# Low parts of the MLP weights kept in DRAM, MLP sums added on GpSimd, and a written order for GpSimd and SyncE, in an attention block with a token-mixing MLP

## The chip, the cores and the metric

One core of one Trainium2 chip. The metric is the time of one execution on the device in microseconds; the rows below come from one profiled execution, in which times count from the first instruction (the span).

## The reference, cut to what matters

```
x:(1,2048,640)  wqkv:(640,1920)  wo:(640,640)  w1:(2048,1728)  w2:(1728,2048)
g = sigmoid((x * gate_w).sum(-1, keepdims=True))
qkv = x @ wqkv                       # 32 heads of 20
a = softmax(q k^T * 20**-0.5) v @ wo
h = layernorm(x)                     # over the 640 channels
u = gelu(einsum("bsd,sf->bdf", h, w1) + b1)
b = einsum("bdf,fs->bds", u, w2) + b2, transposed back to (1,2048,640)
out = g * a + (1 - g) * b
```

## The kernel before

Every float32 matrix product outside the attention weights is made of float32r parts. A value is split into a high part (a copy to float32r) and a low part (value minus high part) by `hi_lo`, and a product is the sum high x high, high x low, low x high. TensorE's order is written out (`manual_schedule`) for the whole kernel, that of ScalarE and VectorE from L212 to L664. GpSimd and SyncE get an order from the scheduler, which may place their instructions earlier or later than the program does.

The span falls into four parts. First come the projections: q and k are stored to DRAM as high and low parts (`qk_unit`), then v, and the statistics of x. The last 24 units of q and k (loop at L373) already run beside `h_load`, `h_norm` and `h_split`, which normalize x for the MLP, and beside the first four pieces of weights.

Then comes the MLP, `mlp`, in two halves of the channels (d = 0 and 1, 320 channels each). For each of 14 blocks f of the hidden width it makes `u` (2048 tokens in, four pieces of weights of four 128x128 tiles each), then for each of 16 blocks t of tokens it makes `y` (four pieces each). Each of the 2592 yields of `mlp` is one step: a pair of matmuls (`pair64`) of 64 contraction rows each, one into each of two PSUM tiles, so a result is the sum of two PSUM tiles. `u_evac` has ScalarE copy the first, and five steps later VectorE adds the second (L411); then ScalarE makes the gelu and the high part, GpSimd the low part. `y_evac` does the same with a scale and a bias (L438, L441) and has SyncE store the result to `y_d`.

The list `w_list` names the weights twice over, once for each half, 120 pieces for each. `w_need(k)` loads pieces up to k+8 on SyncE (`w_raw`, eight buffers) and splits pieces up to k+3 (`w_split`, five buffers of each part): the high part on ScalarE, the low part on GpSimd.

Meanwhile TensorE and VectorE also run a stream of score tiles (`s_tiles`), which finds the maximum of each row of scores before the softmax: a matmul into one of three PSUM buffers `s` and a VectorE reduction (L148) per tile, 128 tiles for each pair of heads p. 736 of the 2048 tiles are run within the MLP, evenly over its steps. After each 64 tiles the reductions are joined in four VectorE instructions in a row (L151 to L157) and stored to `m_d`. At the first tile of p, a hook (`start_ahead`) loads the stack of q and k rows for p+1 (`base_stack`: 18 loads), and at p = 4, tile 512, also the stack for the attention of p = 0 (20 loads), `load_m` (8) and `load_v` (1).

Then the attention: 16 pairs of heads by 32 iterations. An iteration makes four score tiles (`st_op`), a ScalarE exponential on each (L646), the products with v of the iteration before (`pv_flush`), and takes 0, 2 or 3 tiles of the stream between them. Last come the output projection and the store.

Of the kernel before, what the change touches and what calls it, by code (L numbers as in the profile page):

```python
# [7 lines left out]
F32 = mybir.dt.float32  # L8
F32R = mybir.dt.float32r
# [19 lines left out]
def gated_mix(ctx, tc, xT, x, wqk, wv0, wv1, wo, w1, w1t, b1, w2, b2, out):  # L29
# [63 lines left out]
    omg = cp.tile([P, NT], F32, name="omg")  # L93
    b2o = cp.tile([P, NT], F32, name="b2o")

    def load_stack(p, ks, qs, full):
        for j in range(2):
            r0 = 64 * j
            h = 2 * p + j
            rows = slice(DH * h, DH * h + DH)  # L100
            kf = ks.bitcast(F32)
            nc.sync.dma_start(kf[r0: r0 + DH, :], k_d[0, rows, :])
            nc.sync.dma_start(kf[r0 + DH: r0 + 2 * DH, :], k_d[0, rows, :])
            nc.sync.dma_start(kf[r0 + 2 * DH: r0 + 3 * DH, :], k_d[1, rows, :])
            if full:
                nc.sync.dma_start(kf[r0 + 3 * DH: r0 + 3 * DH + 2, :], ones)
            for i in range(2):
                qf = qs[i].bitcast(F32)
                cols = slice(i * (S // 2), (i + 1) * (S // 2))
                nc.sync.dma_start(qf[r0: r0 + DH, :], q_d[0, rows, cols])  # L110
                nc.sync.dma_start(qf[r0 + DH: r0 + 2 * DH, :], q_d[1, rows, cols])
                nc.sync.dma_start(qf[r0 + 2 * DH: r0 + 3 * DH, :], q_d[0, rows, cols])

    def base_stack(p, full):
        ks = k8([P, S], F32R, f"ks{p}_{full}")
        qs = [q4([P, S // 2], F32R, f"qs{p}_{full}_{i}") for i in range(2)]
        load_stack(p, ks, qs, full)
        return ks, qs

    def load_m(p, qs):  # L120
# [10 lines left out]
    def load_v(p):  # L131
        v_tiles[p] = base.tile([P, NT, NPAIR], F32, tag="v", bufs=2, name=f"v{p}")
        c0 = NPAIR * (p % 8)
        nc.sync.dma_start(v_tiles[p], v_d[p // 8, :, :, c0: c0 + NPAIR].rearrange("t p c -> p t c"))

    def s_tiles(p):
        for half in range(2):
            mx = cp.tile([P, 4, 2, 8], F32, tag="mx", bufs=2, name=f"mx{p}_{half}")
            for t in range(8):
                for kc in range(4):  # L140
                    for j in (1, 0):
                        def f(j=j, kc=kc, t=t):
# [7 lines left out]
            mm = cp.tile([P, 16], F32, tag="mm", bufs=2, name=f"mm{p}_{half}")  # L150
            nc.vector.tensor_reduce(mm, mx.rearrange("p k j t -> p (j t) k"), axis=AX.X, op=OP.max)  # L151
            mc = cp.tile([P, 32], F32R, tag="mc", bufs=2, name=f"mc{p}_{half}")
            mt = cp.tile([P, 32], F32, tag="mt", bufs=2, name=f"mt{p}_{half}")
            nc.vector.tensor_scalar_mul(mc[:, :16], mm, -1.0)
            nc.vector.scalar_tensor_tensor(mc[:, 16:], mm, -1.0, mc[:, :16].bitcast(F32),
                                           op0=OP.mult, op1=OP.subtract)
            nc.vector.transpose(mt, mc.bitcast(F32))  # L157
            m_queue[0].dma_start(m_d[p, half], mt)
# [168 lines left out]
    for _ in range(2):  # L327
        for f in f_order:
            for c in range(4):
                w_list.append((w1t[:, 4 * c: 4 * c + 4], True) if f == FF else (w1[f][:, 4 * c: 4 * c + 4], False))  # L330
        for t in range(NT):
            for c in range(4):
                w_list.append((w2[t][:, 4 * c: min(4 * c + 4, FT)], False))
    AHEAD = 4
    w_tmp = [k8([P, 16, P], F32R, f"wtmp{i}") for i in range(2)]
    w_raws, w_got = [], []
# [36 lines left out]
    for n, (m, q) in enumerate(units):  # L373
        if q == 0 and n + 4 < len(units):
            w[units[n + 4][0]] = load_w(units[n + 4][0])
        if n == 19:
            s_src[0] = base_stack(0, False)
# [9 lines left out]
        if n in (18, 19):  # L387
            w_split(n - 18)
            w_raw(n - 16)
        qk_unit(m, w[m], q)  # L390
        if n in (20, 21):
            w_split(n - 18)
    p1s.close()

    gps = ExitStack()
# [12 lines left out]
    def u_evac(f, d, ps, gh, gl):  # L408
        xg = gp.tile([P, HALF], F32, tag="xg", bufs=3, name=f"xg{d}_{f}")
        nc.scalar.activation(xg, ps[0], AF.Copy)  # L410
        soon.append([5, lambda: nc.vector.tensor_add(xg, ps[1], xg)])  # L411
        if f == FF:
            soon.append([6, lambda: u_swap(d, xg)])
# [8 lines left out]
    def u_swap(d, xg):  # L422
        sw = gp.tile([P, HALF], F32, tag="sw", bufs=1, name=f"sw{d}")
        nc.gpsimd.dma_start(sw[:TL], xg[TL:])
        nc.gpsimd.dma_start(sw[TL:], xg[:TL])
        nc.gpsimd.tensor_add(xg, xg, sw)

    def u_tail(f, d, xg, gh):
        nc.scalar.activation(xg, xg, AF.Gelu_apprx_tanh, bias=b1_t[:, f:f + 1])
# [5 lines left out]
    def y_evac(t, d, ps):  # L435
        ty = hp.tile([P, HALF], F32, tag="ty", bufs=3, name=f"ty{d}_{t}")
        c = slice(t, t + 1)
        nc.scalar.activation(ty, ps[0], AF.Identity, bias=b2o[:, c], scale=omg[:, c])  # L438

        def rest():  # L440
            nc.vector.scalar_tensor_tensor(ty, ps[1], omg[:, c], ty, op0=OP.mult, op1=OP.add)  # L441
            nc.sync.dma_start(y_d[t * P:(t + 1) * P, d * HALF:(d + 1) * HALF], ty)

        soon.append([5, rest])

    def mlp(hs):
        k = 0
# [59 lines left out]
    for n, _ in enumerate(steps):  # L507
        settle()
        while done + 2 <= S_AHEAD and done < S_AHEAD * (n + 1) / STEPS:
            for _ in range(2):  # L510
                next(stream)()
            done += 2
    settle(True)
    while done < S_AHEAD:
        next(stream)()
        done += 1
    gps.close()
    hps.close()
# [13 lines left out]
            s_src[p + 1] = s_stack(p + 1)  # L532

    hooks[0] = start_loop
    m_queue[0] = nc.gpsimd
    s_src[6] = s_stack(6)

    def norm_steps(h0, h1):
# [82 lines left out]
    for p in range(NP):  # L621
# [3 lines left out]
        for it in range(32):  # L625
# [23 lines left out]
            due = min((p * 32 + it + 1) * LEFT // (NP * 32 - 38) + 1, LEFT)
            take = min(due - given, 3)  # L650
            for n in range(4):
                st_op((n + turn) % 2, n // 2, s_tile if n == 0 and take < 3 else st_tile)
                if n < take:
                    next(stream)()
            given += take
            if take and given == LEFT:
                next(stream, None)
# [83 lines left out]
```

## Time and profile before

| | us |
|---|---|
| median of three runs | 1918.32 (1918.08 to 1920.92) |
| profiled execution, its own time | 1924.69 |
| span of the profiled execution | 1922.9 |
| TensorE busy in the span | 1878.7 (98%) |
| VectorE busy | 1463.1 (76%) |
| ScalarE busy | 1335.4 (69%) |
| GpSimd busy | 557.5 (29%) |

The matmuls' ends are modelled, so a busy share of TensorE near 100% is not its peak rate. Each of the four parts of the span has its own limit, and the shares of the whole span mix them.

### The profile page before, as it was taken

To read this page: it belongs to the slowest core of one execution; us is meant where nothing else is said; L and a number is where in the kernel's file an instruction comes from. 1 tells how busy PE (TensorE), PEld (TensorE's weight loads), DVE (VectorE), ACT (ScalarE), POOL (GpSimd) and SP (SyncE) were. 2 spreads that over 40 slices of the span, in tenths; PEclk is the share of its full clock that TensorE was granted. 3 is DMA by queue.
4 is the path that set the end of the run, shared out by engine and by line. 5 is a ranking of instruction groups with operands and counts; after the bars stand their busy time and mean duration, and the time that the engine had idled before them with its cause. 6 is when DMAs were issued, how large, how long until landed. Compare 5 with 4: busy or idle time off the path is not lost. (4 is left out here: it accounts for less than half of the span.)

```text
span 1922.9 us, 39183 instructions
## 1 busy us (share of the span) xinstructions
PE 1878.7 (98%) x14978; PEld 1162.0 (60%) x14978; DVE 1463.1 (76%) x2465; ACT 1335.4 (69%) x2595; POOL 557.5 (29%) x731
## 2 busy tenths in 40 slices
PE   9999889999999999999999999999999999999998
PEld 7998788998999996333333333333333333333378
DVE  4202388999999997888888888888888888886127
ACT  4253233343443335999999999999999999999930
POOL 1024266667776562210110101001220012111210
PEclk9999899999999998999999999999999999999999
DMA  8467775556655563315040404231542134211263
GB/s 282 139 198 220 208 180 153 148 162 175 171 141 142 163 177 93 80 40 113 7 97 12 99 16 89 53 84 24 107 101 69 32 76 99 48 34 52 70 217 134
DMA packets 153742, 216.63 MB, mean 113 GB/s; under 512 B 66783, under 2 KB 92991, under 8 KB 149647
## 3 DMA queue, kind: packets, MB, share of 16 engines
q1 hardware_dynamic: 136336, 186.96, 36.6%
q0 software_dynamic: 13472, 18.63, 4.3%
q10 hardware_dynamic: 3744, 8.52, 1.3%
q8 instruction: 118, 1.93, 0.5%
q14 instruction: 72, 0.58, 0.1%
HBM read 165.43 MB, written 48.25 MB: 111 GB/s over the span
## 5 line engine op out<-in xcount | busy, mean ns | idle before, releaser
L148 DVE TENSOR_REDUCE mx<-s 128x1 f32<-128x512 f32 x2048 | 1283.5, 683 | 168.8 <-PE s L146 149.5
L646 ACT ACTIVATE p<-st 128x512 f32<-128x512 f32 x2048 | 1050.8, 620 | 41.1 <-PE s L146 14.7
L643 PEld LDWEIGHTS st<-qs_True,ks_True 62*128 62x128 f32 x2048 | 326.5, 185 | 476.0 <-ACT p L646 229.8
L643 PE MATMUL st<-qs_True,ks_True 62*128 62x512 f32 x2048 | 606.5, 424 | 1.2 <-ACT p L646 0.8
L586 PE MATMUL pv<-p,v 128*32 128x512 f32 x4096 | 550.1, 606 | 0.0
L146 PE MATMUL s<-sk,sq 60*128 60x512 f32 x1280 | 442.2, 440 | 2.6 <-DVE mx L148 2.6
L41 POOL TENSOR_TENSOR wl<-wr,wh 128x512 fp32r<-128x512 f32 x228 | 271.8, 1215 | 117.4 <-ACT wh L38 100.2
L146 PE MATMUL s<-ks_False,qs_False 60*128 60x512 f32 x768 | 253.3, 411 | 11.7 <-DVE mx L148 11.7
L573 POOL DMA_DIRECT2D o_d<-oev x128 | 66.5, 519 | 611.4 <-DVE oev L567 593.3
L38 ACT ACTIVATE wh<-wr 128x512 fp32r<-128x512 f32 (+2 forms) x246 | 139.9, 594 | 137.0 <-PE y L46 50.4
L146 PEld LDWEIGHTS s<-sk,sq 60*128 60x128 f32 x1280 | 208.5, 184 | 21.6 <-DVE mx L148 12.7
L46 PE MATMUL y<-gh,wh 64*128 64x320 f32 x896 | 208.6, 310 | 0.0
L46 PE MATMUL u<-hh,wh 64*128 64x320 f32 x864 | 199.7, 310 | 4.4 <-ACT wh L38 4.4
L46 PE MATMUL y<-gh,wl 64*128 64x320 f32 x832 | 200.5, 310 | 2.7 <-POOL wl L41 2.7
L46 PE MATMUL y<-gl,wh 64*128 64x320 f32 x832 | 202.6, 310 | 0.0
L46 PE MATMUL u<-hl,wh 64*128 64x320 f32 x864 | 199.1, 309 | 0.0
L46 PE MATMUL u<-hh,wl 64*128 64x320 f32 x800 | 188.1, 311 | 4.5 <-POOL wl L41 4.5
L586 PEld LDWEIGHTS pv<-p,v 128*32 128x32 f32 x4096 | 83.0, 108 | 173.8 <-issue 162.1
L46 PEld LDWEIGHTS y<-gh,wh 64*128 64x128 f32 x896 | 154.3, 187 | 0.4
L146 PEld LDWEIGHTS s<-ks_False,qs_False 60*128 60x128 f32 x768 | 138.3, 188 | 24.9 <-DVE mx L148 23.4
L46 PEld LDWEIGHTS u<-hh,wh 64*128 64x128 f32 x864 | 150.0, 188 | 4.8 <-ACT wh L38 4.6
L46 PEld LDWEIGHTS u<-hl,wh 64*128 64x128 f32 x864 | 150.8, 188 | 0.3
(112 smaller groups left out, 1837.4 us busy)
## 6 DMA issues: line engine op xcount, KB each, us to landing
wr<-in_w_dram SPq DMA_DIRECT2D x200, 256.0 KB
qs_True<-q_d SPq DMA_DIRECT2D x192, 80.0 KB
ks_True<-k_d SPq DMA_DIRECT2D x96, 160.0 KB
sk<-k_d SPq DMA_DIRECT2D x60, 160.0 KB
sq<-q_d SPq DMA_DIRECT2D x120, 80.0 KB
qs_False<-q_d SPq DMA_DIRECT2D x72, 80.0 KB
ks_False<-k_d SPq DMA_DIRECT2D x36, 160.0 KB
v_d<-vt SPq DMA_DIRECT2D x32, 168.0 KB
```

The source lines that it names most:

```text
L38: nc.scalar.activation(hi, src, AF.Copy)
L41: (lo_eng or nc.vector).tensor_sub(lo, src, hi.bitcast(F32))
L46: nc.tensor.matmul(ps[k], a[r], b[r], start=start, stop=stop)
L146: nc.tensor.matmul(ps, qs[half][r, t * P:(t + 1) * P], ks[r, kc * 512:(kc + 1) * 512], start=True, stop=True)
L148: nc.vector.tensor_reduce(mx[:, kc, j, t: t + 1], ps, axis=AX.X, op=OP.max)
L573: nc.gpsimd.dma_start(o_d[DH * h: DH * h + DH, cols], ev[r: r + DH, :])
L586: nc.tensor.matmul(pv[r: r + 32, :], v_tiles[p][:, kt, 10 * j: 10 * j + 32], pts[j, c], start=(kt == 0), stop=(kt == NT - 1))
L643: nc.tensor.matmul(ps, ks[r, kt * P:(kt + 1) * P], qs[qh][r, c * 512:(c + 1) * 512], start=True, stop=True)
L646: nc.scalar.activation(pt, ps, AF.Exp, scale=SCALE)
```

## The change

ScalarE copies both PSUM tiles of an MLP sum to SBUF, and GpSimd adds the copies. In the second half of the channels, h_norm runs on ScalarE in two instructions. GpSimd, SyncE too, follow the program's order from the start of the projections' last loop to the end of the attention. In the first half, ScalarE's queue stores each low part of the weights to a DRAM tensor `lo_d`; in the second half SyncE loads it from there, and GpSimd makes none. The stores of `y_d` go to ScalarE's queue, 24 steps after the evacuation; those of `m_d` to GpSimd's. The joining of 64 reductions is spread: two tiles later the reduction on VectorE and negation and split on GpSimd, eight tiles later the transposition on VectorE. The loads of the first stack and the first four pieces go to GpSimd's queue, those of the stack for p = 1 to tile 48. In the attention, iterations that take two tiles of the stream order them differently, and the stream ends six iterations earlier.

```
 base_stack(p, full, eng=nc.sync), load_stack likewise: all loads go to eng
+def s_max(p, half, mx):
+    nc.vector.tensor_reduce(mm, mx.rearrange("p k j t -> p (j t) k"), axis=AX.X, op=OP.max)
+    nc.gpsimd.tensor_scalar_mul(mm, mm, -1.0)
+    hi_lo(mc[:, :16], mc[:, 16:], mm, hi_eng=nc.gpsimd, lo_eng=nc.gpsimd)
+    s_close.append([8, lambda: s_store(p, half, mc)])
+def s_store(p, half, mc):
+    nc.vector.transpose(mt, mc.bitcast(F32))
+    s_close.append([M_LAG[0], lambda: m_queue[0].dma_start(m_d[p, half], mt)])
+def s_next():          # replaces next(stream)(): runs one tile, then what of s_close is due
 s_tiles, after 64 tiles: the four VectorE instructions and the store give way to
+            s_close.append([2, lambda p=p, half=half, mx=mx: s_max(p, half, mx)])
-    m_queue = [nc.sync]
+    m_queue = [nc.gpsimd]
     pvs.close()
+    ordered.enter_context(tc.manual_schedule(engines={EG.Pool, EG.SP}))
 h_norm:
+        if d:
+            nc.scalar.activation(xm, xm, AF.Identity, bias=negm[:, t:t + 1])
+            nc.scalar.activation(xm, xm, AF.Copy, scale=rstd[:, t:t + 1])
+            return
+    lo_d = dram.tile([PER, P, 4, P], F32, name="lo_d")        # PER = 120
 w_raw:
-        nc.sync.dma_start(raw[:, :n, :m], src)
+        (nc.gpsimd if k < AHEAD else nc.sync).dma_start(raw[:, :n, :m], src)
 w_split:
+        elif k < PER:
+            hi_lo(hi[:, :n], lo[:, :n], raw[:, :n], hi_eng=nc.scalar, lo_eng=nc.gpsimd)
+            stores.append((lo_d[k, :, :n], lo[:, :n].bitcast(F32)))
         else:
-            hi_lo(hi[:, :n], lo[:, :n], raw[:, :n], hi_eng=nc.scalar, lo_eng=nc.gpsimd)
+            nc.scalar.activation(hi[:, :n], raw[:, :n], AF.Copy)
+            nc.sync.dma_start(lo[:, :n].bitcast(F32), lo_d[k - PER, :, :n])
 w_need:
+        while len(stores) > (0 if len(w_got) >= PER else 2):
+            nc.scalar.dma_start(*stores.pop(0))
 loop over units: the first splits one or two units later, after qk_unit at n == 19
+            s_src[0] = base_stack(0, False, nc.gpsimd)
 u_evac:
         nc.scalar.activation(xg, ps[0], AF.Copy)
-        soon.append([5, lambda: nc.vector.tensor_add(xg, ps[1], xg)])
+        x2 = half_sum(ps[1], 1.0)                # ScalarE copy, scaled
+        soon.append([6, lambda: nc.gpsimd.tensor_add(xg, xg, x2)])
-            soon.append([10, lambda: u_gelu(f, xg, gh, gl)])
+            soon.append([18, lambda: u_gelu(f, xg, gh, gl)])
 y_evac:
+        x2 = half_sum(ps[1], omg[:, c])
-            nc.vector.scalar_tensor_tensor(ty, ps[1], omg[:, c], ty, op0=OP.mult, op1=OP.add)
-            nc.sync.dma_start(y_d[t * P:(t + 1) * P, d * HALF:(d + 1) * HALF], ty)
-        soon.append([5, rest])
+            nc.gpsimd.tensor_add(ty, ty, x2)                     # after 6 steps
+            nc.scalar.dma_start(y_d[t * P:(t + 1) * P, d * HALF:(d + 1) * HALF], ty)   # after 24
 start_ahead:
-        if 1 <= p + 1 < 6:
+        if 2 <= p + 1 < 6:
             s_src[p + 1] = base_stack(p + 1, False)
 loop over steps:
+            if done == 48:
+                s_src[1] = base_stack(1, False)
 attention:
-            due = min((p * 32 + it + 1) * LEFT // (NP * 32 - 38) + 1, LEFT)
+            due = min((p * 32 + it + 1) * LEFT // (NP * 32 - 44) + 1, LEFT)
             for n in range(4):
-                st_op((n + turn) % 2, n // 2, s_tile if n == 0 and take < 3 else st_tile)
-                if n < take:
-                    next(stream)()
+                j = n // 2 if take == 2 else n % 2
+                st_op((j + turn) % 2, n % 2 if take == 2 else n // 2, s_tile if n == 0 and take < 3 else st_tile)
+                if n < take if take != 2 else n % 2 == 0:
+                    s_next()
```

## Rows read from the trace of the kernel before

**Rows 1.** Windows by stage: length, busy us by engine, granted clock, DMA share, GB/s
```profile
219.00:310.00 91.00, 74.83 (x810) 70.41 (x810) 67.49 (x114) 29.63 (x56) 47.34 (x47) 0.89 0.71 190
310.00:367.00 57.00, 56.05 (x697) 54.64 (x695) 56.71 (x97) 21.86 (x42) 36.77 (x31) 1.00 0.55 143
367.00:489.00 122.00, 115.53 (x1404) 110.51 (x1402) 117.01 (x201) 46.44 (x91) 82.36 (x83) 1.00 0.58 167
489.00:618.00 129.00, 127.19 (x1579) 124.31 (x1577) 128.38 (x224) 52.29 (x103) 93.02 (x85) 1.00 0.57 153
618.00:745.00 127.00, 123.63 (x1484) 119.70 (x1481) 122.78 (x211) 42.32 (x79) 69.45 (x62) 0.97 0.50 139
760.00:1800.00 1040.00, 1037.39 (x7150) 404.53 (x7154) 852.99 (x1419) 1002.17 (x1951) 161.95 (x303) 1.00 0.29 63
```

**Rows 2.** Timeline of TensorE in a quiet stretch of the second half's u
```profile
604.14 0.31 PE L46 MATMUL u<-hh,wh 64*128 64x320 f32 x1
...
604.80 0.31 PE L46 MATMUL u<-hh,wh 64*128 64x320 f32 x1
```

**Rows 3.** Groups of VectorE by line: busy us, mean ns of one
```profile
L148 DVE TENSOR_REDUCE mx<-s 128x1 f32<-128x512 f32 x2048 | 1283.5, 683 | 168.8 <-PE s L146 149.5 <-PE st L643 15.8
L441 DVE SCALAR_TENSOR_TENSOR ty<-y,omg,ty 128x320 f32<-128x320 f32 x32 | 17.4, 542 | 0.7 <-ACT ty L438 0.7
L411 DVE TENSOR_TENSOR xg<-u,xg 128x320 f32<-128x320 f32 x28 | 13.5, 482 | 6.9 <-ACT xg L410 6.9
```

**Rows 4.** Timelines of VectorE and TensorE where 64 tiles are joined
```profile
675.83 0.27 DVE L151 TENSOR_REDUCE mm<-mx 128x16 f32<-128x64 f32 x1
...
676.55 0.21 DVE L157 STREAM_TRANSPOSE mt<-mc 128x32 f32<-128x32 f32 x1
676.68 3.74 DVE L148 TENSOR_REDUCE mx<-s 128x1 f32<-128x512 f32 x6
...
677.38 0.50 PE L146 MATMUL s<-ks_False,qs_False 60*128 60x512 f32 x1 [0.53 <-DVE mx L148]
```

**Rows 5.** Waits in 310 to 745: us in total, times, longest
```profile
PEld s L146 <- DVE mx L148: 19.7, 43, 2.8
...
PEld y L46 <- POOL wl L41: 3.6, 4, 2.0
```

**Rows 6.** Waits in 225 to 300 and 278 to 310; clock in 224 to 234
```profile
ACT wh L38 <- DMA wr<-in_w_dram: 23.2, 5, 9.7
...
PE u L46 <- DVE evl L41: 5.5, 1, 5.5
...
PE u L46 <- ACT wh L38: 4.4, 1, 4.4
...
PE u L46 <- POOL wl L41: 3.8, 1, 3.8
...
224.00:234.00 10.00, 7.70 (x50) 7.15 (x52) 5.75 (x9) 2.31 (x4) 1.29 (x1) 0.52 0.61 206
```

**Rows 7.** Groups of GpSimd and ScalarE in the MLP by line
```profile
L41 POOL TENSOR_TENSOR wl<-wr,wh 128x512 fp32r<-128x512 f32 x228 | 271.8, 1215 | 117.4 <-ACT wh L38 100.2 <-DMA wr<-in_w_dram 14.0 <-DMA m_d<-mt 3.1
L41 POOL TENSOR_TENSOR gl<-xg,gh 128x320 fp32r<-128x320 f32 x26 | 22.8, 878 | 16.6 <-PE s L146 12.2 <-ACT gh L38 4.4
L438 ACT ACTIVATE ty<-y,b2o,omg 128x320 f32<-128x320 f32 x32 | 19.8, 619 | 91.8 <-PE y L46 79.7 <-PE s L146 12.0
L410 ACT ACTIVATE xg<-u 128x320 f32<-128x320 f32 x28 | 12.2, 436 | 94.1 <-PE u L46 83.0 <-PE s L146 11.1
```

**Rows 8.** SyncE's issues by line (min/median/max ns); a GpSimd load's us to landing
```profile
L110 SPq DMA_DIRECT2D qs_True<-q_d x64: 272/273/1768, 549.2 to 1679.4; - x64
L127 SPq DMA_DIRECT2D qs_True<-m_d x128: 639/640/3907, 555.6 to 1768.7; - x128
L345 SPq DMA_DIRECT2D wr<-in_w_dram x232: 322/328/1675, 191.0 to 719.0; - x116
xn<-in_x_dram POOLq DMA_DIRECT2D x16, 320.0 KB, 4.1
```

**Rows 9.** The window with the densest DMA, columns as in the first group
```profile
10.00:20.00 10.00, 10.00 (x41) 8.14 (x41) 8.29 (x14) 7.47 (x14) 0.00 (x0) 0.91 0.98 340
```

**Rows 10.** Timelines of VectorE and ScalarE around one joining in the attention
```profile
1267.88 0.27 DVE L151 TENSOR_REDUCE mm<-mx 128x16 f32<-128x64 f32 x1
...
1268.60 0.21 DVE L157 STREAM_TRANSPOSE mt<-mc 128x32 f32<-128x32 f32 x1
...
1271.63 4.83 ACT L646 ACTIVATE p<-st 128x512 f32<-128x512 f32 x9 [0.82 <-PE s L146]
```

More of the change, by code (lines that the diff above doesn't have):

```diff
@@ L94, in gated_mix, with load_stack @@
     b2o = cp.tile([P, NT], F32, name="b2o")
-    def load_stack(p, ks, qs, full):
+    def load_stack(p, ks, qs, full, eng=nc.sync):
         for j in range(2):
@@ L101, in load_stack @@
             kf = ks.bitcast(F32)
-            nc.sync.dma_start(kf[r0: r0 + DH, :], k_d[0, rows, :])
-            nc.sync.dma_start(kf[r0 + DH: r0 + 2 * DH, :], k_d[0, rows, :])
-            nc.sync.dma_start(kf[r0 + 2 * DH: r0 + 3 * DH, :], k_d[1, rows, :])
+            eng.dma_start(kf[r0: r0 + DH, :], k_d[0, rows, :])
+            eng.dma_start(kf[r0 + DH: r0 + 2 * DH, :], k_d[0, rows, :])
+            eng.dma_start(kf[r0 + 2 * DH: r0 + 3 * DH, :], k_d[1, rows, :])
             if full:
-                nc.sync.dma_start(kf[r0 + 3 * DH: r0 + 3 * DH + 2, :], ones)
+                eng.dma_start(kf[r0 + 3 * DH: r0 + 3 * DH + 2, :], ones)
             for i in range(2):
@@ L109, in load_stack, with base_stack @@
                 cols = slice(i * (S // 2), (i + 1) * (S // 2))
[L110 to L114, printed above, removed]
+                eng.dma_start(qf[r0: r0 + DH, :], q_d[0, rows, cols])
+                eng.dma_start(qf[r0 + DH: r0 + 2 * DH, :], q_d[1, rows, cols])
+                eng.dma_start(qf[r0 + 2 * DH: r0 + 3 * DH, :], q_d[0, rows, cols])
+    def base_stack(p, full, eng=nc.sync):
         ks = k8([P, S], F32R, f"ks{p}_{full}")
         qs = [q4([P, S // 2], F32R, f"qs{p}_{full}_{i}") for i in range(2)]
-        load_stack(p, ks, qs, full)
+        load_stack(p, ks, qs, full, eng)
         return ks, qs
@@ L134, in load_v, with s_finish @@
         nc.sync.dma_start(v_tiles[p], v_d[p // 8, :, :, c0: c0 + NPAIR].rearrange("t p c -> p t c"))
+    s_close = []
+    def s_max(p, half, mx):
+        mm = cp.tile([P, 16], F32, tag="mm", bufs=2, name=f"mm{p}_{half}")
+        mc = cp.tile([P, 32], F32R, tag="mc", bufs=2, name=f"mc{p}_{half}")
+        nc.vector.tensor_reduce(mm, mx.rearrange("p k j t -> p (j t) k"), axis=AX.X, op=OP.max)
[3 more added lines that the diff above has]
+    def s_store(p, half, mc):
+        mt = cp.tile([P, 32], F32, tag="mt", bufs=2, name=f"mt{p}_{half}")
+        nc.vector.transpose(mt, mc.bitcast(F32))
+        s_close.append([M_LAG[0], lambda: m_queue[0].dma_start(m_d[p, half], mt)])
+    M_LAG = [8]
+    def s_next():
+        next(stream)()
+        for e in list(s_close):
+            e[0] -= 1
+            if e[0] <= 0:
+                s_close.remove(e)
+                e[1]()
+    def s_finish():
+        next(stream, None)
+        while s_close:
+            s_close.pop(0)[1]()
     def s_tiles(p):
@@ L149, in s_tiles @@
                         yield f
[L150 to L158, printed above, removed]
+            s_close.append([2, lambda p=p, half=half, mx=mx: s_max(p, half, mx)])
     def s_stream(on_start):
@@ L333, in gated_mix @@
                 w_list.append((w2[t][:, 4 * c: min(4 * c + 4, FT)], False))
+    PER = len(w_list) // 2
+    lo_d = dram.tile([PER, P, 4, P], F32, name="lo_d")
     AHEAD = 4
     w_tmp = [k8([P, 16, P], F32R, f"wtmp{i}") for i in range(2)]
-    w_raws, w_got = [], []
+    w_raws, w_got, stores = [], [], []
     def w_raw(k):
@@ L386, in gated_mix @@
             w_raw(1)
-        if n in (18, 19):
-            w_split(n - 18)
-            w_raw(n - 16)
+        if n in (19, 20):
+            w_split(n - 19)
+            w_raw(n - 17)
         qk_unit(m, w[m], q)
-        if n in (20, 21):
-            w_split(n - 18)
+        if n == 19:
+            s_src[0] = base_stack(0, False, nc.gpsimd)
+        if n in (22, 23):
+            w_split(n - 20)
     p1s.close()
@@ L410, in u_evac, with half_sum @@
         nc.scalar.activation(xg, ps[0], AF.Copy)
-        soon.append([5, lambda: nc.vector.tensor_add(xg, ps[1], xg)])
+        x2 = half_sum(ps[1], 1.0)
+        soon.append([6, lambda: nc.gpsimd.tensor_add(xg, xg, x2)])
         if f == FF:
-            soon.append([6, lambda: u_swap(d, xg)])
+            soon.append([7, lambda: u_swap(d, xg)])
+            soon.append([30, lambda: nc.gpsimd.tensor_add(xg, xg, sws.pop())])
             soon.append([44, lambda: u_tail(f, d, xg, gh)])
         else:
-            soon.append([10, lambda: u_gelu(f, xg, gh, gl)])
+            soon.append([18, lambda: u_gelu(f, xg, gh, gl)])
+    def half_sum(ps, scale):
+        x2 = gp.tile([P, HALF], F32, tag="x2", bufs=2, name="x2")
+        nc.scalar.activation(x2, ps, AF.Copy, scale=scale)
+        return x2
+    sws = []
     def u_gelu(f, xg, gh, gl):
@@ L425, in u_swap @@
         nc.gpsimd.dma_start(sw[TL:], xg[:TL])
-        nc.gpsimd.tensor_add(xg, xg, sw)
+        sws.append(sw)
     def u_tail(f, d, xg, gh):
@@ L438, in y_evac, with store @@
         nc.scalar.activation(ty, ps[0], AF.Identity, bias=b2o[:, c], scale=omg[:, c])
+        x2 = half_sum(ps[1], omg[:, c])
         def rest():
-            nc.vector.scalar_tensor_tensor(ty, ps[1], omg[:, c], ty, op0=OP.mult, op1=OP.add)
-            nc.sync.dma_start(y_d[t * P:(t + 1) * P, d * HALF:(d + 1) * HALF], ty)
-        soon.append([5, rest])
+            nc.gpsimd.tensor_add(ty, ty, x2)
+        def store():
+            nc.scalar.dma_start(y_d[t * P:(t + 1) * P, d * HALF:(d + 1) * HALF], ty)
+        soon.append([6, rest])
+        soon.append([24, store])
     def mlp(hs):
@@ L514, in gated_mix @@
     while done < S_AHEAD:
-        next(stream)()
+        s_next()
         done += 1
@@ L534, in gated_mix @@
     hooks[0] = start_loop
-    m_queue[0] = nc.gpsimd
+    M_LAG[0] = 0
     s_src[6] = s_stack(6)
@@ L647, in st_op @@
                 pts[j, c] = pt
[L649 removed]
+            due = min((p * 32 + it + 1) * LEFT // (NP * 32 - 44) + 1, LEFT)
             take = min(due - given, 3)
             for n in range(4):
[L652 to L654 removed]
+                j = n // 2 if take == 2 else n % 2
+                st_op((j + turn) % 2, n % 2 if take == 2 else n // 2, s_tile if n == 0 and take < 3 else st_tile)
+                if n < take if take != 2 else n % 2 == 0:
+                    s_next()
             given += take
             if take and given == LEFT:
[L657 removed]
+                s_finish()
             turn = (turn + take) % 2
```

2 lines of the change are left out of this document (removed).

## The prediction

> **What bounds the kernel now.** I read the windows by stage first, then the waits of each stage, then timelines where waits repeat. The page's 98% for TensorE is no guide, since matmul ends are modelled; so I look for the engine next to it in each stage. From 310 to 745, most of the MLP, VectorE is busy in 56.71 + 117.01 + 128.38 + 122.78 = 424.9 of 435 us, 98%; ScalarE stands near 40% and GpSimd between 55 and 72% [rows 1]. TensorE could go faster there: in a quiet stretch ten matmuls start within 0.66 us, 0.147 us to a step of two [rows 2], while the 129 us of the second half's u hold 656 steps, 0.197 us each. Some 190 score tiles run in between, but part of the difference is waiting: the weight loads of the score tiles wait 19.7 us for VectorE's reductions, and y waits 3.6 us for GpSimd's low parts [rows 5]. The longest of these repeat every 64 tiles: the four joining instructions take VectorE from 675.83 to 676.68, and TensorE stands 0.53 us behind them [rows 4].
>
> The start of the MLP, 219 to 310, is another matter: 74.83 of 91 us busy at a granted clock of 0.89 [rows 1]. Three single waits of 5.5, 4.4 and 3.8 us make 13.7 us. ScalarE waits 23.2 us for weights there, and after the first wait the clock is at 0.52, so mostly at 1.2 GHz, for 10 us [rows 6].
>
> The attention is different again: ScalarE is busy in 1002 of 1040 us, VectorE in 853 [rows 1]. ScalarE loses 0.82 us once per joining, right after VectorE's four instructions [rows 10]; there are 21 joinings in this part, since 1312 of 2048 tiles remain.
>
> **The change part by part**, against the profiled execution's own 1924.7 us, of which the span is 1922.9.
>
> *(a) The MLP's start.* The first stack leaves SyncE for GpSimd, the second waits for tile 48, and the weights have SyncE nearly to themselves; the first splits come a unit or two later, so that ScalarE doesn't stand at them with a projection's evacuation behind it. The three waits are all of this kind. They cost 13.7 us, and the clock costs (1 - 0.89) x 91 = 10.0 us of work [rows 1, 6]: 23.7 us to be had. Nothing new takes their place but 18 issues on GpSimd; a GpSimd load lands after 4.1 us [rows 8], and the pieces are issued two units ahead of their splits. I take -20; the ends are 0 and -23.7.
>
> *(b) The MLP from 310 on.* VectorE loses 28 adds of 0.482 and 32 of 0.542 us [rows 3] and, in 11 joinings, the two instructions between L151 and L157, which take 676.55 - 676.10 = 0.45 us [rows 4]: 13.5 + 17.4 + 5.0 = 36 us, about 32 of them after 310. That is the most that can come back. The visible waits, 19.7 + 3.6 = 23.3 us [rows 5], and half of the clock's loss in the last stage ((1 - 0.97) x 127 / 2 = 2) are what I count on: -24, ends 0 and -32. The work goes to engines with room. GpSimd pays 60 adds at 0.878 = 53 us, and loses in the second half 116 low parts at 1.215 = 141 us [rows 7]. In y of the first half it loses 16 norms and gains 16 adds: near 75% as before. ScalarE pays 28 x 0.436 + 32 x 0.619 = 32 us for copies, 32 x 0.619 = 20 us for norms [rows 7] and 148 issues at 0.33 = 49 us [rows 8]: from 163 to 264 of 435 us. The fullest stage, 367 to 489, goes from 46 to about 100 of 122. What is late if that cover goes is the next wh, which is made three pieces ahead.
>
> *(c) SyncE's order at tile 512.* In the program's order, the hook at tile 512 issues everything in one go: 18 loads for p = 5, 20 + 8 + 1 for the attention's first stack. At 0.27 to 0.33 us plus 0.07 between them, and 0.64 plus 0.07 for the eight [rows 8], that is 39 x 0.37 + 8 x 0.71 = 20 us in which no weights are issued. Tile 512 falls in the second half (368 tiles belong to the first), where low parts come from SyncE too. High parts aren't the trouble: raw pieces are issued eight ahead. Low parts are issued three ahead into five buffers, so SyncE gets to the hook when TensorE ends piece k-2, with five pieces (60 steps at 0.18 with their score tiles, 10.8 us) still in store. The first low part behind the hook lands after 20 + 0.8 + some 3.5 us [rows 8]. TensorE stands 24.3 - 10.8 = 13.5 us, and if the clock falls afterwards as it does in [rows 6] it loses 3 to 5 more: +17, ends 0 (the loads don't go out in this order) and +20. The hook at tile 384 has 18 loads alone, 6.7 + 0.8 + 3.5 = 11 us against 10.8: nothing.
>
> *(d) More DMA.* Low parts are 108 x 256 KB = 28.3 MB, stored once and loaded once: 56.6 MB more on the same DMA engines. The MLP uses 0.71 x 91 + 0.55 x 57 + 0.58 x 122 + 0.57 x 129 + 0.50 x 127 = 304 us of all engines' time [rows 1]. The addition costs 163 us at the densest window's rate (340 GB/s at a share of 0.98) [rows 9], 197 us at that of 367 to 489 (167 at 0.58) [rows 1]: 467 to 501 us in all, where (a) and (b) leave 526 - 44 = 482 us and (c) makes 499. So DMA gets nearly full. With five to eight pieces in store I take +10 for late pieces; ends 0 and +30. The Trainium skill's page "DMA: Bandwidth & Descriptors", section "Issuing engines are not separate DMA queues", speaks against this part: DMAs of all issuing engines interleave on the same 16 engines, and another queue saves issue time alone. By that rule, moving stores off SyncE is worth no bandwidth, and the 56.6 MB count in full; that is the second rival below.
>
> *(e) The attention.* Of the four joining instructions two stay on VectorE, apart from each other, 0.27 and 0.21 us [rows 10], in iterations of some 2.1 us of which VectorE is idle 18% [rows 1]: they fit. 21 x 0.82 = 17.2 us; I take -15, ends 0 and -17. The transposition now waits for GpSimd, eight tiles (6 us) after its instructions were queued; what is queued behind it on VectorE are reductions, and for these TensorE waits. GpSimd's stores of 0.5 us don't fill 6 us. The new order within iterations that take two tiles leaves each matmul with a partner on the other 64 rows: 0, ends -8 and +8 (some 90 iterations by 0.09 us). Ending six iterations earlier moves work but adds none: 0.
>
> Sum: -20 - 24 + 17 + 10 - 15 = -32, 1892.7 us for a profiled execution. The median of the runs shown lies 6.4 us below the profiled one: **1886 us**.
>
> **Rivals.** *SyncE's burst does not stall*: (c) is 0 and little of (d) is left: -32 - 17 - 2, 1867. For it: before, the same loads went out from 590 on without a visible wait, but low parts did not need SyncE then. *DMA sets the MLP's pace*: 501 us and the rest of the burst, (d) at its end of +30: -12, 1906. For it the shares above; against it 340 GB/s once reached, and 256 KB pieces over all partitions, the kind that goes fastest. *VectorE was not the bound*: (b) is 0 and only (a) and (e) come: -8, 1910; against it 98% busy and the waits in [rows 5]. *Slower*: low parts run dry all through the MLP, because DMA handles the added bytes worse than anything shown: at 220 GB/s of full time they cost 257 us, the MLP 561 instead of 526, and with (e) the sum is +20, 1938. It decides from (541 - 304) = 237 us, 239 GB/s, downward; the stage at 0.50 and 139 GB/s [rows 1] stands at 278.
>
> **How the numbers follow.** The forecast has 0.42, no stall 0.20, DMA-paced 0.20, VectorE not the bound 0.06, slower 0.12. Of the cases below 1918, some 0.04 reach the neighbourhood of no change, so: faster by over 0.2% (3.8 us, about what a measurement of this kernel can tell) 0.84, within 0.2% 0.03, slower 0.13. The range goes from 1856, where (a) and (b) come nearly whole beside no stall, to 1924, past the DMA-paced case with a smaller (e) and into the first part of the slower one; the likeliest case's own range is 1872 to 1900.
>
> **What would show it.** (a): 219 to 310 shorter by some 20 us, no granted clock near 0.5 there. (b): no L411 and L441 on VectorE, its waits in [rows 5] down to a few us, u of the second half near 120 us but for the burst. (c): at two thirds of the second half's u a gap of TensorE of some 13 us that waits for the load of a low part, with SyncE issuing stacks. (d): DMA share from 0.9 up, and waits for wl or wh spread over all pieces. (e): no gaps of 0.8 us after L151. Wrong it would be if GpSimd or ScalarE, now in a fixed order with TensorE's evacuations behind them, held up PSUM, or if low parts came late at each piece.

## The result, and the profile after

The changed kernel takes 1928.45 us (median of 20 runs, 1921.92 to 1934.72); the kernel before, run beside it, 1919.51 (1913.67 to 1927.25). The ratio is 1.0043, interval 1.0031 to 1.0055: slower by 0.4%, where 1886 and faster was forecast. The profiled execution took 1934.27, its span 1932.5.

First the windows of the changed kernel by stage, columns as in [rows 1]. Its MLP runs from 219.1 to 761.8 (219.7 to 744.8 before); the stages begin at 219.1, 355.6, 480.2 and 645.3 (before 219.7, 367.1, 495.4 and 618.1).

```profile
219.00:310.00 91.00, 80.49 (x953) 78.34 (x954) 75.97 (x122) 35.86 (x71) 66.44 (x70) 0.92 0.84 259
310.00:355.00 45.00, 43.44 (x545) 42.39 (x543) 42.67 (x70) 19.96 (x40) 34.52 (x34) 1.00 0.87 273
355.00:482.00 127.00, 122.44 (x1508) 120.68 (x1507) 117.17 (x192) 70.05 (x143) 97.88 (x105) 0.97 0.89 288
...
499.00:512.00 13.00, 2.16 (x19) 1.81 (x18) 1.42 (x4) 2.62 (x6) 2.97 (x4) 0.61 0.85 188
512.00:594.00 82.00, 82.00 (x1021) 81.30 (x1019) 79.92 (x131) 35.67 (x73) 22.59 (x33) 0.98 0.78 236
594.00:626.00 32.00, 2.73 (x25) 2.38 (x23) 2.23 (x4) 0.00 (x0) 0.61 (x1) 0.56 0.60 151
...
646.00:762.00 116.00, 116.00 (x1473) 115.60 (x1470) 114.44 (x188) 48.13 (x94) 18.70 (x29) 1.00 0.79 249
...
1576.00:1590.00 14.00, 10.22 (x59) 4.17 (x59) 7.49 (x12) 7.58 (x16) 4.94 (x8) 0.76 0.50 118
```

The first half of the MLP got shorter by 14.6 us (275.7 to 261.1), the second longer by 32.2 (249.4 to 281.6). Two windows do it: in 499 to 512 and 594 to 626 TensorE works 4.9 of 45 us. The other engines are nearly idle there too, and the DMA share is 0.60 in the longer one, less than in the busy stretches on either side. In between TensorE waits for nothing: 82.00 of 82.00 and 116.00 of 116.00.

The waits (what, total us, times, longest) of 200 to 310, 310 to 482, 482 to 660 and 770 to 1840 name the releasers:

```profile
PE s L176 <- DMA qs_False<-q_d: 7.8, 1, 7.8
...
PE y L46 <- ACT wh L38: 4.1, 1, 4.1
...
PE u L46 <- DMA wl<-lo_d: 41.3, 3, 29.3
...
PE st L693 <- DMA qs_True<-m_d: 4.7, 2, 3.8
```

The rows of [rows 5] have all but gone, but 41.3 us of waiting for low parts that SyncE loads have come. TensorE's timeline shows the first wait and the two long ones:

```profile
227.28 0.80 PE L176 MATMUL s<-ks_False,qs_False 60*128 60x512 f32 x2 [7.78 <-DMA qs_False<-q_d]
...
510.68 0.64 PE L46 MATMUL u<-hh,wl 64*128 64x320 f32 x2 [10.84 <-DMA wl<-lo_d]
...
624.31 0.63 PE L46 MATMUL u<-hh,wl 64*128 64x320 f32 x2 [29.27 <-DMA wl<-lo_d]
```

And SyncE's timeline (start, length, line, what is loaded), first at tile 384, then at tile 512:

```profile
489.84 0.44 SPq L394 DMA_DIRECT2D wl<-lo_d  x1
490.33 0.36 SPq L102 DMA_DIRECT2D ks_False<-k_d  x1
490.74 0.32 SPq L103 DMA_DIRECT2D ks_False<-k_d  x1
491.11 0.35 SPq L104 DMA_DIRECT2D ks_False<-k_d  x1
496.24 0.27 SPq L110 DMA_DIRECT2D qs_False<-q_d  x1
...
504.41 0.40 SPq L374 DMA_DIRECT2D wr<-in_w1t_dram  x1
505.58 0.34 SPq L394 DMA_DIRECT2D wl<-lo_d  x1
...
583.84 0.33 SPq L394 DMA_DIRECT2D wl<-lo_d  x1
584.22 0.36 SPq L102 DMA_DIRECT2D ks_False<-k_d  x1
...
611.10 0.27 SPq L112 DMA_DIRECT2D qs_True<-q_d  x1
612.17 5.61 SPq L127 DMA_DIRECT2D qs_True<-m_d  x8
617.82 0.45 SPq L134 DMA_DIRECT2D v<-v_d  x1
...
619.69 0.43 SPq L394 DMA_DIRECT2D wl<-lo_d  x1
```

A load's own length is 0.27 to 0.36 us, as in [rows 8]. But the 38 loads of stacks from 584.22 to 612.17 take 27.95 us, 0.735 us each: between them SyncE waits, mostly for loads of ks and qs some places earlier. From the last low part ahead of the hook to the first behind it 35.85 us pass, and at tile 384, 15.74 us. Of these 15.74, 4.8 are one wait, before 496.24, for a store of `y_d`; the last section comes back to it.

### The profile page after: what moved, and what is told of

It reads as the page before. It is cut to its first block, busy times and chain, and to the rows that moved or that the text cites. A ratio compares the mean times of both kernels' runs of the same rounds, so it can differ in the third digit from the quotient of the medians.

```text
span 1932.5 us, 39337 instructions
## 1 busy us (share of the span) xinstructions
PE 1854.8 (96%) x14978; PEld 1148.3 (59%) x14978; DVE 1428.0 (74%) x2341; ACT 1366.8 (71%) x2687; POOL 503.5 (26%) x788
## 5 line engine op out<-in xcount | busy, mean ns | idle before, releaser
L176 PE MATMUL s<-ks_False,qs_False 60*128 60x512 f32 x768 | 216.9, 403 | 7.8 <-DMA qs_False<-q_d 7.8
L46 PE MATMUL u<-hh,wl 64*128 64x320 f32 x800 | 149.0, 313 | 42.7 <-DMA wl<-lo_d 41.3
L46 PE MATMUL u<-hh,wh 64*128 64x320 f32 x864 | 158.6, 311 | 2.9 <-ACT wh L38 2.9
L46 PE MATMUL u<-hl,wh 64*128 64x320 f32 x864 | 158.4, 310 | 0.0
L38 ACT ACTIVATE wh<-wr 128x512 fp32r<-128x512 f32 (+2 forms) x130 | 73.6, 594 | 102.6 <-DMA wr<-in_w_dram 29.5
L46 PEld LDWEIGHTS y<-gh,wl 64*128 64x128 f32 x832 | 144.1, 186 | 1.5 <-POOL wl L41 1.1
L41 POOL TENSOR_TENSOR wl<-wr,wh 128x512 fp32r<-128x512 f32 x112 | 134.2, 1213 | 41.1 <-ACT wh L38 16.9
L46 PEld LDWEIGHTS y<-gl,wh 64*128 64x128 f32 x832 | 144.3, 186 | 0.1
L46 PEld LDWEIGHTS u<-hh,wl 64*128 64x128 f32 x800 | 99.6, 190 | 45.3 <-DMA wl<-lo_d 42.3
```

The lines of the kernel that those rows point to most:

```text
L38: nc.scalar.activation(hi, src, AF.Copy)
L41: (lo_eng or nc.vector).tensor_sub(lo, src, hi.bitcast(F32))
L46: nc.tensor.matmul(ps[k], a[r], b[r], start=start, stop=stop)
```

## The experiments

Theory: the loss is the bursts of stack loads in SyncE's fixed order, ahead of low parts that now come through the same queue. Rivals: the added bytes alone make DMA the limit; the fixed order does harm by itself; VectorE was not the bound, so nothing was there to gain. Medians of several runs, and the ratio to the kernel before on the same chip with its interval:

| | us | ratio |
|---|---|---|
| changed kernel | 1928.45 | 1.0043 (1.0031 to 1.0055) |
| e1: stack loads spread, one every 6 steps | 1916.74 | 0.9983 (0.9966 to 1.0001) |
| e2: no reload | 1894.88 | 0.9871 (0.9846 to 0.9897) |
| e3: no written order | 1919.43 | 0.9994 (0.9978 to 1.001) |
| e4: kernel before with the written order alone | 1952.10 | 1.0171 (1.0146 to 1.0196) |
| e5: e1 and e2 together | 1869.75 | 0.9746 (0.9721 to 0.9772) |
| e6: spread, one every 16 steps | 1884.35 | 0.9813 (0.9787 to 0.984) |
| e7: reload, but no stack loads beside it | 1878.91 | 0.9796 (0.9767 to 0.9825) |
| e8: e2 and e3 together | 1892.92 | 0.9863 (0.9838 to 0.9889) |
| e9: e5, first stack earlier, later stacks spread | 1863.63 | 0.9710 (0.9676 to 0.9744) |
| e10: e5 with the MLP's adds back on VectorE | 1877.72 | 0.9790 (0.9749 to 0.983) |
| e11: e5 with the joining back in one go | 1897.40 | 0.9896 (0.9853 to 0.9939) |
| e12: 16 rows a load (one run) | 1946.66 | before: 1920.51 |

**e1, the loads spread.** The hooks' loads go into a list, and the loop over steps takes one out every six steps (code shortened); the eight loads of `load_m` are one item of the list.

```
 load_stack
-            eng.dma_start(dst, src)
+            trickle.append(lambda: eng.dma_start(dst, src))
 loop over steps
+        if trickle and n % 6 == 0:
+            trickle.pop(0)()
```

> The changed kernel with the stack loads of the MLP's hooks (p = 1 to 5 and the attention's first stack) issued one every six steps instead of in one go. Burst theory (SyncE's written order puts 18 or 47 stack loads ahead of the low parts, and these go at some 0.7 us each): the stalls of 29.7 and 11.1 us at u<-hh,wl and some 5 us of smaller ones go, and 5 to 8 us of slow clock with them: 1870 to 1885. Rival, DMA full (56.6 MB more on the same engines): the same bytes still have to move, waits for weights spread over all pieces, 1915 or more. Second rival, the moved adds and copies hold up PSUM: 1925, as the changed kernel.

1916.74: a miss for the burst theory. The number is that of the rival with DMA full. The two long stalls are gone, but 16 waits for low parts have come, 29.7 us in all (TensorE's waits in 215 to 770):

```profile
PE y L46 <- DMA wl<-lo_d: 17.3, 8, 8.6
...
PE u L46 <- DMA wl<-lo_d: 12.4, 8, 5.9
```

They are not spread over all pieces, as that rival had it: all but one end in 490 to 512 and 590 to 650, where stack loads go out. The longest, 8.6 us, ends at 649.46: ahead of it SyncE issues `load_m`'s eight in one go (5.63 us) and then waits 6.2 us for the landings of stores of `y_d`. The second half is 276 us, against 281.6. By rows, a piece of 12 steps takes some 2.2 us (0.18 us a step). In it SyncE now brings 512 KB of weights, 1.54 us at 340 GB/s [rows 9], and two stack loads of 0.73 us each: 3.0 us. By this estimate one load every six steps is still more than fits beside a reload, though the DMA share is no more than 0.74 in 590 to 641.

**e2, no reload.** GpSimd makes the low parts in both halves.

```
-        elif k < PER:
-            hi_lo(hi[:, :n], lo[:, :n], raw[:, :n], hi_eng=nc.scalar, lo_eng=nc.gpsimd)
-            stores.append((lo_d[k, :, :n], lo[:, :n].bitcast(F32)))
         else:
-            nc.scalar.activation(hi[:, :n], raw[:, :n], AF.Copy)
-            nc.sync.dma_start(lo[:, :n].bitcast(F32), lo_d[k - PER, :, :n])
+            hi_lo(hi[:, :n], lo[:, :n], raw[:, :n], hi_eng=nc.scalar, lo_eng=nc.gpsimd)
```

> The changed kernel without lo_d: GpSimd makes the low parts in both halves, nothing is stored or loaded again, the bursts stay. Burst theory: raw pieces are issued eight ahead, some 18 us, so the burst of 14 us at tile 384 is hidden and that of 34 us at tile 512 leaves a stall of about 20 us: 1895 to 1910. DMA full: all stalls go with the bytes, 1870 to 1885. Moved adds: 1925 or more, since GpSimd gets 141 us of work back.

1894.88, at the edge of the burst theory's range. The burst at tile 512 outlasts even the eight raw pieces issued ahead; the row of the waits in 215 to 770:

```profile
PE u L46 <- ACT wh L38: 17.7, 1, 17.7
```

The first half is 246 us here, 261 in the changed kernel.

**e3 and e4, the written order.** e3 is the changed kernel without the line, e4 the kernel before with it and nothing else.

```
     pvs.close()
-    ordered.enter_context(tc.manual_schedule(engines={EG.Pool, EG.SP}))
```

> The changed kernel without the written order for GpSimd and SyncE (one line). Burst theory: the scheduler puts weights between stack loads again, the two long stalls shrink to a few us, 1880 to 1905. DMA full: as the changed kernel, 1920 to 1930.

> The kernel before with that one line added and nothing else: GpSimd and SyncE in the program's order. Burst theory: a stall of some 20 us at tile 512 (34 us of loads against 18 us of pieces in store), less some us of waits at the MLP's start: 1920 to 1940. DMA full: no bytes are added, so within 0.5% of before or faster, 1905 to 1922.

1919.43 and 1952.10: both are slower than the burst theory had it. The order alone costs 33 us: in e4 SyncE issues stacks from 594.94 to 628, and TensorE waits 21.4 us at 612 for high parts (its waits in 215 to 775).

```profile
PE u L46 <- ACT wh L38: 24.7, 2, 21.4
```

Without the order (e3) the MLP takes 517 us, but in the attention TensorE waits once 19.6 us for VectorE at 775. So the line does harm in the MLP and good behind it; taking it away settles nothing.

**e5, both.** 

> The changed kernel with both: stack loads one every six steps, and no lo_d (GpSimd makes the low parts in both halves). Theory now: a stack load (20 rows) is slow in itself, some 0.7 us each in a row, so neither the order alone nor the bytes alone stall TensorE, but the stacks together with two weight loads for each piece; one weight load leaves room. Then no stall on weights is left in the MLP: 1870 to 1880, 15 to 25 us under the run without lo_d alone. Rival, each part costs on its own and adds up: spreading gains the same 12 us here as it did with lo_d, 1883.

1869.75, just below the range. TensorE's only wait of over 0.8 us in the MLP is 4.2 us for the first stack. Its windows:

```profile
219.00:310.00 91.00, 84.39 (x1020) 80.56 (x1020) 80.40 (x130) 37.28 (x76) 68.25 (x70) 0.98 0.64 171
465.00:700.00 235.00, 235.00 (x2975) 234.42 (x2973) 232.45 (x381) 104.25 (x211) 187.42 (x195) 1.00 0.57 156
```

The whole second half, 235.3 us, is without a gap at full clock. GpSimd, which makes the low parts again, is busy 187 of 235 us and late for nothing. e1 saves 12 us, e2 34, both 59: the bursts and the reload cost most where they meet.

**e6 and e7, the reload kept.** e6 has one load every 16 steps, and the eight of `load_m` one by one. e7 keeps the reload and leaves out the stack loads of p = 1 to 5: their score tiles use the stack of p = 0; the attention's first stack is loaded at tile 256.

```
 e6
-        if trickle and n % 6 == 0:
+        if trickle and n % 16 == 0:
 e7
-            s_src[p + 1] = base_stack(p + 1, False)
-        if p == 4:
+            s_src[p + 1] = s_src[0]
+        if p == 2:
             st_src[0] = base_stack(0, True)
```

> The changed kernel, lo_d kept, stack loads one every sixteen steps instead of six, load_m's eight too. Theory of stacks together with reloads: at a third of the rate the two loads of a piece and the stacks fit, the waits for low parts shrink from 35 us to under 12, 1885 to 1900. Rival, reloading low parts is late by itself whatever the stacks do: 1915 as at six steps.

> The changed kernel, lo_d kept, that leaves out the stack loads of p = 1 to 5 (all score tiles within the MLP use the stack of p = 0, the output is then not the reference's) and loads the attention's first stack at tile 256, in the first half. Theory of stacks together with reloads: in the second half no stall on low parts is left, its u and y take 230 to 240 us instead of 282. Rival, the reload by itself: stalls of some 30 us remain in the second half. The first half may stall up to 15 us at the moved burst. Total 1875 to 1895 against 1910 or more.

1884.35, just below its range, and 1878.91, within it, both as the theory had it. e7's second half is 236.9 us, with 0.7 us of waiting for low parts (its waits in 215 to 770); e6's 244.4 with 5.0.

```profile
PE u L46 <- DMA wl<-lo_d: 0.7, 1, 0.7
```

So the reload is nearly free where nothing stands in front of it in the queue. By the arithmetic of e1, one load every 16 steps makes 1.54 + 0.55 = 2.1 us of loads to 2.2 of work, and DMA is nearly full, as these windows of e6 show:

```profile
474.00:719.00 245.00, 239.93 (x2990) 235.75 (x2988) 234.00 (x382) 105.65 (x212) 54.09 (x80) 0.99 0.91 268
590.00:660.00 70.00, 69.21 (x876) 68.55 (x874) 67.84 (x111) 30.70 (x61) 12.22 (x19) 1.00 0.97 280
```

e6 still loses 15 us to e5; its first half, where low parts are stored, takes 255.5 us against 245.4. In e7 the burst that was moved to the first half stalls TensorE there, 12.2 us at 406.

**e8, no reload and no order.** 

> The changed kernel without lo_d and without the written order of GpSimd and SyncE: what the moved adds, the spread joinings and the rest give with the scheduler's order. If the moved work alone is good for some 35 us, as predicted, 1880 to 1890, unless the scheduler's order stalls the attention as in the run without the written order (20 us): then 1900. Rival, the gain of the run without lo_d came from the written order: 1915.

1892.92. The MLP is free of the burst, and the attention has its wait again, 15 us at 748.

**e9, e10, e11.** All start from e5. e9 loads the first stack two units earlier and spreads the score stacks of the attention; e10 and e11 each put one part back on VectorE.

```
 e9
-        if n == 19:
+        if n == 17:
-        load_stack(p, ks, qs, False)
+        load_stack(p, ks, qs, False, slow=True)
 e10, in u_evac; y_evac likewise
-        x2 = half_sum(ps[1], 1.0)
-        soon.append([6, lambda: nc.gpsimd.tensor_add(xg, xg, x2)])
+        soon.append([5, lambda: nc.vector.tensor_add(xg, ps[1], xg)])
 e11, in s_tiles
-            s_close.append([2, lambda p=p, half=half, mx=mx: s_max(p, half, mx)])
+            nc.vector.tensor_reduce(mm, mx.rearrange("p k j t -> p (j t) k"), axis=AX.X, op=OP.max)
+            nc.vector.tensor_scalar_mul(mc[:, :16], mm, -1.0)
+            nc.vector.scalar_tensor_tensor(mc[:, 16:], mm, -1.0, mc[:, :16].bitcast(F32),
+                                           op0=OP.mult, op1=OP.subtract)
+            nc.vector.transpose(mt, mc.bitcast(F32))
```

> The best so far (stack loads one every six steps, no lo_d), with the first stack asked for two units earlier (before unit 18 instead of 20) and the attention's score stacks spread too, up to two loads an iteration. The first score tile's wait of 4.2 us at the MLP's start and the wait of 2 to 4 us for load_m at p = 12 should go: 1860 to 1868. If the attention's stacks never mattered beyond that one place: 1866.

> The same base as the run with spread loads and no lo_d (1869.75), with the adds of the MLP's sums back on VectorE, as before the change. If VectorE was the bound, 28 x 0.482 + 32 x 0.542 = 31 us come back on it: +15 to +28, 1885 to 1898. If the MLP is TensorE's by now, within 5 us of the base.

> The same base, with the four joining instructions back on VectorE in a row. In the attention 21 x 0.8 = 17 us come back, in the MLP 11 gaps of 0.7 to 1 us: +20 to +28, 1890 to 1898. If VectorE's slack hides them now: within 5 us of the base.

e9, 1863.63, has the lowest median; the intervals of its ratio and e5's overlap. The MLP's first score tile no longer waits for its stack (4.2 us in e5); the fourth waits 2.4 us for VectorE instead. e10, 1877.72, lies between its two expectations. Its ratio is above e5's by 0.0044, about as much as the two intervals leave open; its profile has an MLP of 490.6 us where e5 has 480.7. e11's is above by 0.0150, 29 us, as expected; its MLP takes 500.6, and its attention, from the first exponential to the last, 1088.2 where e5 has 1078.6. In 310 to 700 of e11 this wait is back:

```profile
PE s L184 <- DVE mx L186: 13.1, 9, 2.6
```

So VectorE was the bound, and the joining was the dearer part by far. What makes it so dear stands on VectorE's timeline of e11, and beside it GpSimd's:

```profile
439.75 0.27 DVE L189 TENSOR_REDUCE mm<-mx 128x16 f32<-128x64 f32 x1
440.05 1.13 DVE L192 TENSOR_SCALAR mc<-mm 128x16 fp32r<-128x16 f32 x1
441.21 1.18 DVE L193 SCALAR_TENSOR_TENSOR mc<-mm,mc 128x16 fp32r<-128x16 f32 x1
442.43 0.21 DVE L195 STREAM_TRANSPOSE mt<-mc 128x32 f32<-128x32 f32 x1
```

```profile
438.60 3.77 POOL L41 TENSOR_TENSOR wl<-wr,wh 128x512 fp32r<-128x512 f32 x3
```

The two small instructions, 0.18 and 0.17 us in the stretch of [rows 4], take 1.13 and 1.18 here. GpSimd's three instructions of 1.26 us end near 439.9, 441.1 and 442.4, and VectorE's two end at 441.2 and 442.4: each lasts until GpSimd's is done. Of the 22 such instructions in e11's MLP 13 are held in this way, of the 22 in the kernel before, where GpSimd has no adds to make, 7.

**e12, 16 rows a load.** At tiles 384 and 512 each load of 20 rows is made with 16; the other four rows of all of them follow in loads of their own (code shortened).

```
+            eng.dma_start(dst[r: r + 16, :], src[:16])
+            tails.append(lambda: eng.dma_start(dst[r + 16: r + DH, :], src[16:]))
```

> The changed kernel, but at tiles 384 and 512 each load of 20 rows of q or k is made as one of 16 rows, and the remaining 4 rows of all of them are loaded behind, in as many loads again. What it tells: the rate at which SyncE gets through the first 18 loads at tile 384 and the first 36 at tile 512, which was 0.73 us each with 20 rows at a DMA share of 0.60 to 0.65. Theory one, a load of 20 rows keeps ten of the 16 DMA engines busy and these ten are full: 16 rows use all 16, so a load takes 0.73 x 16/20 x 10/16 = 0.37 us, about the issue itself, and the first 36 loads at tile 512 take 13 to 16 us, with a DMA share well over 0.65. Theory two, a load waits for the landing of the one eight before it and a landing takes its 5 to 6 us whatever the size: about 0.7 us each again, 25 us for 36, with the share falling rather than rising. The whole time is no verdict here, since the 4-row loads come on top; by either theory it is at or above that of the changed kernel, some 1925 to 1960 us.

Neither theory. The first 38 loads at tile 512 take 24.65 us (588.53 to 613.18), 0.65 us each, nearly as the second had it; but the DMA share rises, as the first had it, while GB/s fall. The burst in the changed kernel, then in e12 the burst and the loads of four rows, with the lines of SyncE's timeline at which they begin and end:

```profile
584.00:612.00 28.00, 11.04 (x139) 10.68 (x135) 12.23 (x22) 4.07 (x9) 2.99 (x6) 0.74 0.66 158
...
588.00:613.00 25.00, 11.36 (x144) 11.00 (x140) 12.57 (x22) 4.36 (x9) 3.00 (x6) 0.83 0.89 146
...
613.00:627.00 14.00, 0.00 (x0) 0.00 (x0) 0.00 (x0) 0.00 (x0) 0.00 (x0) 0.50 0.21 60
...
588.53 2.18 SPq L100 DMA_DIRECT2D ks_False<-k_d  x3
...
613.18 1.62 SPq L102 DMA_DIRECT2D ks_False<-k_d  x3
...
627.43 5.62 SPq L134 DMA_DIRECT2D qs_True<-m_d  x8
```

The 36 loads of four rows take 14.25 us, 0.40 each, hardly above their issue. So a load with a fifth of the rows still costs over half the time: in this one run the number of loads counts for more than their bytes. Why an engine is busy so long with one row is not settled by these runs.

## Why the prediction was wrong

**(c) is the step that failed, by its size.** The place was right (two thirds into the second half's u, TensorE waiting for a low part while SyncE issues stacks), the store in hand was right (TensorE stops 10.8 us after the hook; 10.8 forecast), and so was the landing (4.6 us; 4.3). Wrong was "39 x 0.37 + 8 x 0.71 = 20 us in which no weights are issued": the time of an issue was taken for that of a load. Issued back to back the loads went through at 0.735 us each, and the burst, from its start to the first low part behind it, took 35.5 us: 35.5 + 4.6 - 10.8 = 29.3 us of stall instead of 13.5. At tile 384 the stall is 10.8, where "nothing" was forecast; there the time that SyncE takes holds the 4.8 us of waiting for a store of `y_d`, which the sum did not have. The trace of before did hold the figure. In its attention SyncE gets through 38 stack loads in a row, from the first line here to the second, in 25.68 us, 0.676 each:

```profile
1564.85 0.28 SPq L102 DMA_DIRECT2D sk<-k_d  x1
...
1590.53 0.39 SPq L134 DMA_DIRECT2D v<-v_d  x1
```

The reading that "before, the same loads went out from 590 on without a visible wait" was not a test of the burst: from 590.47 on only 14 stack loads and four of `load_m` go out before 18 loads of weights. Behind the two stalls the granted clock was 0.97 (510.70 to 595) and 0.91 (624.30 to 646), 2 to 2.5 us of work lost each time where 3 to 5 were forecast.

**(d) was right in its statement, too small in effect.** The DMA share is 0.84 to 0.89 through the first half, and 0.91 where the reload runs freely (e6). The stores cost 5 us in the first half where they are the only difference (250 in e1, 245.4 in e5), 15 beside bursts (261.1 in the changed kernel, 246 in e2). But the rival *DMA sets the MLP's pace* falls: e7 reloads all low parts with 0.7 us of waiting. And it is not the added bytes that fill the two stalls, since the share is lower than in any busy stretch of the MLP while SyncE works through the stacks (the 0.85 of 499 to 512 comes from the weights behind them):

```profile
500.00:505.00 5.00, 0.00 (x0) 0.00 (x0) 0.20 (x1) 2.21 (x6) 2.97 (x4) 0.70 0.64 150
...
595.00:612.00 17.00, 0.04 (x1) 0.00 (x0) 1.23 (x2) 0.00 (x0) 0.00 (x0) 0.57 0.63 148
```

Where reload and stacks overlap, e1 shows that loads one at a time do not fit either: 29.7 us of waits for low parts, where 10 were forecast. The result came out on the side of the rival *Slower*, but not by its mechanism: that needed DMA to move less than 239 GB/s at a full share, and e6 moves 268 at 0.91, 294 at a full one. (c) and (d) together were put at 27 us; between the changed kernel and e5 lie 65 us of span: 16 in the first half, 46 in the second, 4 behind. Neither carries the loss alone: of the 59 us between the medians, e1 gets back 12 without the bursts and e2 34 without the reload.

**(a)** came as forecast but for one new wait. u of the first half takes 128.7 us in e5 against 147.4, -19; -20 was forecast. In the changed kernel it takes 136.5, since "Nothing new takes their place but 18 issues on GpSimd" did not hold: the first stack is late by 7.8 us in GpSimd's queue (by 4.2 in e5, which issues it in the same place), and the clock is at 0.67 in that wait. Loaded two units earlier (e9), it is in time.

**(b)** had the right sum with the wrong parts. The three later stages take 128.3, 122.7 and 126.7 us before, and 116.4, 118.7 and 116.6 in e5: -26, forecast -24. But the joining was put at 5 us of it, the adds at the rest; by one profile each, e11 gives 20 us of the MLP to the joining, e10 10 to the adds. That the sum came out so well is in part luck. The one joining that was read in [rows 4] is one with GpSimd idle. Over the MLP of the kernel before, the two instructions take twice as long (groups of VectorE in 219 to 745):

```profile
L155 DVE SCALAR_TENSOR_TENSOR mc<-mm,mc 128x16 fp32r<-128x16 f32 x11 | 4.4, 402 | 0.4
L154 DVE TENSOR_SCALAR mc<-mm 128x16 fp32r<-128x16 f32 x11 | 3.9, 359 | 0.4
```

In e11, beside the moved adds, they take 652 and 654 ns, so its 20 us are likely more than the joining cost before.

**(e)** was right: the attention, from its first exponential to its last, takes 1091.9 us before, 1078.6 in e5 (-13; forecast -15), and the gaps of [rows 10] are gone; e11 gives 9.7 of the 13 back. In the changed kernel it takes 1082.5: at 1576 the loads of `load_m` stand behind 18 stack loads in SyncE's order, the same fault as (c). The 0 for iterations that take two tiles missed a gain: their median, from one's first exponential to the next one's, went from 2038 to 1924 ns (92 of them), while that of those that take three went from 2130 to 2143 (376).

With (a), (b) and (e) at -58 against -59 forecast, e5 lies 48 us below the kernel before in its median, 55.5 in its profile: the gains were real, and the two bursts with the reload took back all of them and a little more. The norms on ScalarE, the stores of `y_d` in the other queue and the order within iterations had no run of their own; what each is worth stays open.

Three smaller readings of the prediction were off. The 656 steps of the second half's u take 122.7 us, 0.187 each, since the 129 us of [rows 1] begin ahead of that stage. The sum of 23.3 and 2 us is 25, and was taken as 24. And the rival without a stall says that little of (d) is left, but takes off 2 of its 10 us.

## What to carry to other kernels

When a queue's order is fixed, price everything in front of the urgent load by what a run of such loads took back to back in the trace, not by the length of an issue; then compare that with the work in store. A transfer added to a queue should be tested for what stands in front of it there, not only for its bytes: the same reload made the second half 2 us longer (e7 against e5) or 41 (e1 against e5), by what else was in the queue. And before counting VectorE's time for small instructions, look at their longest cases too: one occurrence may be the cheap one.

## What the runs showed of the hardware that was not expected

**Loads of 20 rows.** A run of them went at 0.735 us each, and the DMA share stood at 0.63 (595 to 612) while nothing else was to do, so a share well under 1 can be all that such loads get. With 16 rows each it stood at 0.89. The Trainium skill, "DMA: Bandwidth & Descriptors", section "Why a DMA increments its semaphore by 16 and not by 1", says that a load is dealt to the largest number of engines up to 16 that divides its rows: ten for 20 rows, 16 for 16. Both shares agree with that; the rate, 0.65 us for 16 rows, does not follow from it.

**One queue waits for another's landing.** At tile 384 SyncE stood 4.8 us before a load of q until a store of y_d had landed (496.24 above), which is in ScalarE's queue and shares no data with it. SyncE's waits in 484 to 513:

```profile
SPq L110 <- DMA y_d<-ty: 4.8, 1, 4.8
```

By the semaphores in the trace, the DMAs of SyncE and ScalarE carry eight of them in turn, and each waits for the DMA that had its semaphore before. So moving a store to the other queue did not take its landing out of the way; in e1, SyncE waits 10.9 us for such landings from 590 to 650.

**VectorE held by GpSimd.** Two 128x16 instructions on SBUF data took 0.175 us with GpSimd idle and up to 1.27 us with it busy, and ended with GpSimd's instruction, while the reductions from PSUM kept their 0.68 us. The Trainium skill, "GPSIMD Engine Reference", section "1. Specifications", names contention of GpSimd with VectorE instructions that read two SBUF inputs or use the two-port mode; the second instruction reads two such inputs, and the trace agrees; the first reads one, and no run shows its mode. Here each was held to the end of an instruction of GpSimd.
